# Half-width second diagonal scores, read back turned, with grouped gate logits and new lags, in a fused attention and mixture-of-experts kernel

## The chip, the cores and the metric

The kernel runs on one core of one Trainium2 chip. The metric is the device time of one execution in microseconds (us), taken as the median of several runs. Lower is better.

## The reference, cut to what matters

For each of 8 batches, with 2496 tokens, a width of 256 and keys of width 64, the attention part is

```python
scores = scale * np.matmul(z, z.transpose(0, 2, 1))
attn = np.maximum(scores, 0.0) ** 2
x = u * np.matmul(attn, v)
```

Queries and keys are the same tensor `z`, so `scores` is symmetric. The second part is a mixture of 8 experts: `logits = x @ w_gate + bias`, the expert is the largest logit, and the output is its probability times `relu(x @ w1[e]) @ w2[e]` with a hidden width of 1024. All values are float32. The kernel splits each float32 operand of a product into a high and a low part in the matmul's reduced format and adds three products.

## The kernel before

**Phase 1 (attention and routing).** The queries of a batch are cut into 5 chunks `c` of 512 (the last has 448), and the keys into 10 key pairs `i` of 2 times 128. A step is one (batch, chunk, key pair). For a step, `scores` makes 6 matmuls from `z` into the one PSUM tile `s` (three pairs; the two matmuls of a pair work on 64 rows of the array each, side by side). ScalarE's `root` (ReLU with the scale) empties `s` into a tile `r`, `square` squares it in place, `high` rounds it to `ah` (on ScalarE or VectorE, as the planner decides), VectorE's `low` takes the rest `al`, and `weigh` makes 24 matmuls with `v` into four banks `acc`. After the last step of a chunk ScalarE's `evacuate_low` (a copy, `x<-acc`) and VectorE's `evacuate_high` empty the banks, `weigh_u` multiplies by `u`, `turn_rows`, `store_rows` and `load_natural` bring the rows into token order through HBM, and `make_gates` makes 8 small matmuls `pg` per chunk (each recorded as two), which `take_gates` turns into the logits `lg`. After the fifth chunk of a batch the tokens are routed and scattered to HBM by expert.

Since scores are symmetric, a block below the diagonal is not computed twice: after a step above the diagonal `turn_squares` (VectorE) turns the squared block, `store_squares` writes it to HBM, and a later chunk reads it with `load_turned` in place of scores, root and square. Steps with `i // 2 == c` are the diagonal: both key pairs of the diagonal were computed at the full 512 queries.

**The order of the work** comes from a planner in the kernel. Each piece of work has an engine, an estimated time, a due step (`need`), and buffers that it takes and drops; the planner plays them through on its own clocks and writes each engine's instructions down in the order that results. All DMAs of phase 1 but the scatters go through SP's one queue in that order. `load_v` and `prep_v_high` (the cast `vh<-vr`) prepare `v` of the next batch while the present one runs.

**Phase 2 (experts)** has its order written out by hand: `up`, `down_both`, `down_high` for tiles of 512 tokens, with weights fetched in quarters into tiles of the pool `x`.

Of the kernel before, what the change touches and what calls it, by code (L numbers as in the profile page):

```python
# [16 lines left out]
P = 128  # L17
# [10 lines left out]
def tile_attention_moe(ctx: ExitStack, tc: tile.TileContext, ut, v, zt, mid, wg, mb, w1, w2, out):  # L28
# [35 lines left out]
    NA = 6  # L64
# [6 lines left out]
    xs = dram.tile([E * CAP, XW], F32, name="xs")  # L71
    natural = {(b, c): dram.tile([P, P // BLK, J, QB], F32, name=f"rows{b}_{c}") for b in range(B) for c in range(NCH)}
# [16 lines left out]
    rows.tile([P, 16], F32, name="room")  # L89
# [58 lines left out]
    def make_blank():  # L148
        t = rows.tile([P, J, XW], F32, tag="x", bufs=NCH + 1, name="blank")
        nc.gpsimd.memset(t, 0.0)  # L150
        blank.append(t)
# [135 lines left out]

    def scores(g, more=False):
# [14 lines left out]
        st_s[g] = s if more or not g else both  # L303

    def root(g):
        w = width[steps[g][1]]
        s = st_s.pop(g)
        r = bulk.tile([P, 2, T], F32, tag="a", bufs=NA, name="r") if g else first_root
# [12 lines left out]
    def turn_squares(g):  # L321

        b, c, i = steps[g]
        y = raw.tile([P, T // QB, 2, QB], F32, tag="turn", bufs=2, name="turn")
# [24 lines left out]
    def split_view(g, x):  # L349

        w = width[steps[g][1]]
        if is_turned(g):
# [3 lines left out]
    def split_out(g, x):  # L356
# [3 lines left out]
        return x.rearrange("p t (x n) -> p t x n", n=QB) if is_turned(g) else x  # L360

    roots = {}

    def square(g):
        w = width[steps[g][1]]
        a = r = st_s.pop(g)
        if g < 2:
# [112 lines left out]
    def evacuate_low(b, c, h):  # L480

        if not h:
            x = oT[b, c] = rows.tile([P, J, XW], F32, tag="x", bufs=NCH + 1, name="x")
# [16 lines left out]
    def turn_rows(b, c, h):  # L500

        if not h:
            pool, tag, n = (rows, "x", NCH + 1) if (b, c) == (B - 1, NCH - 1) else (raw, "turn", 2)
# [13 lines left out]
    def load_natural(b, c):  # L517

        x = X[b, c] = rows.tile([P, J, XW], F32, tag="x", bufs=NCH + 1, name="x")
# [5 lines left out]
    def make_gates(b, c):  # L525

        y = gates[b, c] = bank_tile([P, P], "pg")
        for h in range(KD):
            for j in range(J):
                nc.tensor.matmul(  # L530
                    out=y[j * BLK:(j + 1) * BLK], lhsT=gate_w[:, h], rhs=oT[b, c][:, j, h * P:(h + 1) * P],
                    start=h == 0, stop=h == KD - 1, tile_position=(0, j * BLK),
                )

    def take_gates(b, c):

        if c == 0:
            LG[b] = rows.tile([P, NCOL, BLK], F32, tag="lg", bufs=2, name="lg")
        y = gates.pop((b, c))
        nc.vector.transpose(  # L540
            out=LG[b][:, c * J:(c + 1) * J, :], in_=y.rearrange("p (t i) -> p t i", i=BLK)
        )
        oT.pop((b, c))
# [271 lines left out]
    def fetch_weights(t, quarters=range(4)):  # L815
# [4 lines left out]
        for q in quarters:  # L820
            x = rows.tile([P, F], F32, tag="x", bufs=NCH + 1, name="wr")
# [82 lines left out]

    def piece(on, us, need, f, *args, after=(), take=(), drop=(), gate=-1):
        p = Piece(on, us, need, f, args, [d if isinstance(d, tuple) else (d, 0.1) for d in after if d], list(take), drop, gate)
# [4 lines left out]
        "s": 1, "bank": 6, "a": NA, "ah": DEPTH, "al": DEPTH, "turn": 2, "zm": NCH + 1, "vh": 6, "vl": 6,  # L911
        "zr": 3, "vr": 3, "x": NCH + 1, "u": 1,
    }
    LEAD = 3.6
    LANES = 8
# [19 lines left out]
    def z_pieces(b, c):  # L935
# [5 lines left out]
        high = piece("A", 0.55, need - 1, prep_z_high, b, c, after=[read], take=[hold_z[b, c]], gate=int(need - 4))  # L941
# [627 lines left out]
```

## Time and profile before

| | |
|---|---|
| median of 3 runs | 2137.29 us (2137.05 to 2138.04) |
| profiled execution: its own time | 2140.08 us |
| profiled execution: its span, first to last instruction | 2138.3 us |
| TensorE (PE) busy | 2120.4 us, 99% of the span |
| VectorE (DVE) busy | 1591.4 us, 74% |
| ScalarE (ACT) busy | 1295.9 us, 61% |
| granted TensorE clock over the span | 0.996 |

The profiled execution took 2.8 us longer than the median of the runs, and 1.8 us of it lie outside the span. An engine's busy time counts its own instructions; for PE the ends of matmuls are modelled, since a matmul starts before the one ahead has drained. So what one matmul costs is read from start to start, not from its length.

### The profile page before, as it was taken

The page shows a single profiled execution, that of the slowest core. Times are in us where ns is not written, and L with a number is a line of the kernel's source. Part 1 is how long each engine was busy: PE and PEld are TensorE (multiplying, and loading weights), DVE is VectorE, ACT ScalarE, POOL GpSimd, SP SyncE. Part 2 cuts the span into 40 slices and gives each one's busy share as a digit, 9 for nine tenths or more (in the row PEclk, how much of TensorE's full clock was granted, in tenths as well). Part 3 has the DMA queues.
Part 4 walks back from the last instruction along what each step waited for, and adds up shares of the span by engine and source line. Part 5 has one row for each costly group of instructions (what it writes and reads, how often), then busy time and mean ns, then how long its engine had stood idle before and what let it go on. Part 6 is the DMA issues. An engine that isn't in the chain of part 4 may idle for free.

```text
span 2138.3 us, 42822 instructions
## 1 busy us (share of the span) xinstructions
PE 2120.4 (99%) x15910; PEld 1784.8 (83%) x15910; DVE 1591.4 (74%) x2464; ACT 1295.9 (61%) x1618; POOL 358.2 (17%) x343
## 2 busy tenths in 40 slices
PE   9999999999999999999999999999999999999997
PEld 7878888888888888888888888888888888888886
DVE  8778879878879888888787776666566666656664
ACT  9559668658658567567577643455454545545453
POOL 0001301301301201202104204112121111212112
PEclk9999999999999999999999999999999999999999
DMA  7987977987878878968878765545455454545541
GB/s 181 263 256 169 270 227 171 262 226 179 256 213 202 262 191 216 280 166 224 269 174 227 233 151 152 151 121 159 138 147 150 131 161 120 158 138 148 149 124 41
DMA packets 535403, 398.68 MB, mean 186 GB/s; under 512 B 317968, under 2 KB 469520, under 8 KB 535184
## 3 DMA queue, kind: packets, MB, share of 16 engines
q1 hardware_dynamic: 519968, 354.78, 62.1%
q0 software_dynamic: 15216, 41.08, 5.6%
q8 instruction: 126, 2.06, 0.4%
q14 instruction: 93, 0.76, 0.1%
HBM read 250.68 MB, written 145.16 MB: 185 GB/s over the span
## 4 chain that ended last, share of the span: by engine, by line
PE 97%; ACT 1%; DVE 1%; DMA 0%; issue 0%; POOL 0%; POOLq 0%; SPq 0%; ACTq 0%
PE acc L431 48%; PE ph L1247 19%; PE po L1265 13%; PE s L302 8%; PE po L1271 7%; PE pg L530 1%; ACT r L310 0%; DMA vr<-in_v_dram 0%; ACT r L373 0%; PE warm L1125 0%; DVE hl L1252 0%; PE ph L1345 0%; DMA rows<-turn 0%; ACT ah L396 0%; POOL out_dram L1285 0%
## 5 line engine op out<-in xcount | busy, mean ns | idle before, releaser
L431 PE MATMUL acc<-ah,vh 64*128 64x512 f32 (+1 forms) x3120 | 447.9, 386 | 3.3 <-ACT x L487 2.5
L405 DVE TENSOR_TENSOR al<-r,ah 128x1024 fp32r<-128x1024 f32 (+1 forms) x359 | 421.5, 1182 | 30.7 <-ACT ah L396 26.5
L431 PE MATMUL acc<-al,vh 64*128 64x512 f32 (+1 forms) x3120 | 434.5, 382 | 0.0
L431 PE MATMUL acc<-ah,vl 64*128 64x512 f32 (+1 forms) x3120 | 433.2, 383 | 0.0
L1252 DVE SCALAR_TENSOR_TENSOR hl<-ph,hh 128x512 fp32r<-128x512 f32 x312 | 210.3, 689 | 270.4 <-ACT hh L1251 270.3
L310 ACT ACTIVATE r<-s 128x1024 f32<-128x1024 f32 (+2 forms) x244 | 247.0, 1013 | 250.2 <-PE s L302 247.1
L1247 PE MATMUL ph<-xh,w 128*128 128x512 f32 x1248 | 398.5, 390 | 0.0
L431 PEld LDWEIGHTS acc<-ah,vh 64*128 64x128 f32 x3120 | 303.6, 185 | 67.5 <-issue 7.7
L648 POOL DMA_INDIRECT xs<-x,sloti x160 | 200.7, 1254 | 911.5 <-DMA squares<-turn 394.6
L431 PEld LDWEIGHTS acc<-al,vh 64*128 64x128 f32 x3120 | 307.4, 184 | 51.1
L431 PEld LDWEIGHTS acc<-ah,vl 64*128 64x128 f32 x3120 | 300.5, 185 | 53.0
L1251 ACT ACTIVATE hh<-ph 128x512 fp32r<-128x512 f32 x312 | 181.3, 595 | 264.9 <-PE ph L1247 263.5
L396 ACT CAST ah<-r 128x1024 fp32r<-128x1024 f32 (+1 forms) x268 | 272.9, 1032 | 83.8 <-PE acc L431 47.1
L1265 PE MATMUL po<-w,hh 128*128 128x512 f32 x1248 | 296.2, 389 | 0.0
L1247 PEld LDWEIGHTS ph<-xh,w 128*128 128x128 f32 x1248 | 234.6, 188 | 47.8 <-issue 0.3
L1265 PEld LDWEIGHTS po<-w,hh 128*128 128x128 f32 x1248 | 234.0, 188 | 48.3
L1285 POOL DMA_INDIRECT out_dram<-y,ids x157 | 152.7, 973 | 670.8 <-DVE y L1319 645.4
L329 DVE STREAM_TRANSPOSE turn<-r 128x512 f32<-128x512 f32 x316 | 205.4, 689 | 76.4 <-DMA squares<-turn 42.1
L373 ACT ACTIVATE r<-r 128x1024 f32<-128x1024 f32 (+2 forms) x243 | 255.8, 1053 | 6.7
L1247 PE MATMUL ph<-xl,w 128*128 128x512 f32 x624 | 243.7, 391 | 0.0
L302 PE MATMUL s<-zm 64*128 64x512 f32 (+1 forms) x1452 | 212.2, 392 | 1.8 <-ACT r L310 1.5
L847 DVE TENSOR_TENSOR w<-wr,w 128x1024 fp32r<-128x1024 f32 x148 | 174.5, 1219 | 11.5 <-ACT w L842 11.5
(157 smaller groups left out, 1703.6 us busy)
## 6 DMA issues: line engine op xcount, KB each, us to landing
wr<-in_moe_w_dram SPq DMA_DIRECT2D x148, 512.0 KB
squares<-turn SPq DMA_DIRECT2D x508, 128.0 KB
r<-squares SPq DMA_DIRECT2D x96, 512.0 KB
r<-squares SPq DMA_DIRECT2D x62, 448.0 KB
ut<-in_ut_dram SPq DMA_DIRECT2D x40, 512.0 KB
rows<-turn SPq DMA_DIRECT2D x160, 128.0 KB
x<-rows SPq DMA_DIRECT2D x160, 128.0 KB
xg<-xs SPq DMA_DIRECT2D x156, 128.0 KB
```

The source lines that it names most:

```text
L302: nc.tensor.matmul(out=s[t][:, :w], lhsT=lhs, rhs=mv[halves[t], ql, :w], start=n == 0, stop=n == 2)
L310: nc.scalar.activation(out=r[:, t, :w], in_=s[t][:, :w] if g < 2 else s[:, :, :w], func=AF.Relu, scale=INV)
L329: nc.vector.transpose(out=dst[:, n], in_=src[:, n])
L373: nc.scalar.square(out=a[:, t, :w], in_=r[:, t, :w])
L396: copy(out=split_out(g, ah), in_=split_view(g, st_a[g]))
L405: nc.vector.tensor_tensor(out=split_out(g, al), in0=split_view(g, a), in1=split_out(g, ah).bitcast(F32), op=ALU.subtract)
L431: nc.tensor.matmul(out=acc[b, c][r][dh][:, :w], lhsT=V[b, k // J][y][halves[r], k % J, dh * P:(dh + 1) * P], rhs=x[halves[r], k % 2, :w], ...
L648: nc.gpsimd.indirect_dma_start(out=xs, out_offset=bass.IndirectOffsetOnAxis(ap=RT[b]["sloti"][:n, k:k + 1], axis=0), in_=x[:n, j, :], in_o ...
L1247: nc.tensor.matmul(out=ph, lhsT=lhs, rhs=rhs[:, k, :], start=n == 0, stop=n == 3 * KD - 1)
L1251: nc.scalar.activation(out=hh, in_=ph, func=AF.Relu)
L1252: nc.vector.scalar_tensor_tensor(out=hl, in0=ph, scalar=0.0, in1=hh.bitcast(F32), op0=ALU.max, op1=ALU.subtract)
L1265: nc.tensor.matmul(out=PO[t][j], lhsT=hh, rhs=both, start=f == 0, stop=False, skip_group_check=True)
```

## The change

- **Half diagonal.** On the diagonal of chunks 0 to 3 (all but the very first chunk of the first batch) the second key pair forms scores for 256 queries only. The other 256 columns are the first key pair's block, turned: after the first pair's square, VectorE's `turn_corner` makes two transposes of half size, `store_corner` four DMAs of 64 KB to HBM, and `load_corner` one DMA of 256 KB back into the tile of the second step, into which `root` and `square` then write their half. `order_of` puts the first diagonal pair first among a chunk's fresh steps and the second last.
- **Logits in groups.** `make_gates` and `take_gates` run for chunks (0, 1, 2) and (3, 4) at once; in the last batch for (0), (1), (2, 3) and (4).
- **Accumulation of a chunk's first two steps** is interleaved: first half of step 1, first half of step 2, second half of step 1, second half of step 2 (each half writes two of the four banks).
- **The planner** gets other due times (`LAGS`), waits a little longer for some pieces (`SLACK`), and other estimates. Pools: one `a` tile more (7), three `turn` tiles in place of two, five `x` tiles in place of six.
- For a whole batch the last chunk's turned rows, the routing and the loads of rows come some steps later.

```diff
+        if c < NCH - 1 and (b or c):
+            fresh = [2 * c] + [i for i in fresh if i // 2 != c] + [2 * c + 1]
...
+    def on_diagonal(g, half):
+
+        b, c, i = steps[g]
+        return c < NCH - 1 and i == 2 * c + half and b + c > 0
...
+        q = slice(H, T) if on_diagonal(g, 1) else slice(0, w)
+        n_of = q.stop - q.start
...
-                nc.tensor.matmul(out=s[t][:, :w], lhsT=lhs, rhs=mv[halves[t], ql, :w], start=n == 0, stop=n == 2)
+                nc.tensor.matmul(out=s[t][:, :n_of], lhsT=lhs, rhs=mv[halves[t], ql, q], start=n == 0, stop=n == 2)
...
+        if on_diagonal(g, 1):
+            a = st_a.pop(g)
+            nc.scalar.activation(
+                out=a[:, H // QB:].rearrange("p x t n -> p t x n"),
+                in_=both_of(s)[:, :, 0:H].rearrange("p t (x n) -> p t x n", n=QB), func=AF.Relu, scale=INV,
+            )
...
+    def load_corner(g):
+
+        b, c, i = steps[g]
+        a = st_a[g] = bulk.tile([P, T // QB, 2, QB], F32, tag="a", bufs=NA, name="r")
+        nc.sync.dma_start(out=a[:, 0:H // QB], in_=corners[c, b % 2])
+
+    def turn_corner(g):
+
+        y = raw.tile([P, H // QB, 2, QB], F32, tag="turn", bufs=3, name="turn")
+        dst = y.rearrange("p t r (i n) -> p n r t i", n=2)
+        src = st_a[g][:, :, H:T].rearrange("p n (t i r) -> p n r t i", i=BLK, r=2)
+        for n in range(2):
+            nc.vector.transpose(out=dst[:, n], in_=src[:, n])
...
+    def store_corner(g):
+
+        b, c, i = steps[g]
+        y = st_t.pop(g)
+        dst = corners[c, b % 2].rearrange("(t i) x r n -> i t x r n", i=BLK)
+        for n in range(P // BLK):
+            nc.sync.dma_start(out=dst[:, :, n], in_=y[n * BLK:(n + 1) * BLK])
...
+    def group_of(b, c):
+        splits = ((0, 1, 2), (3, 4)) if b < B - 1 else ((0,), (1,), (2, 3), (4,))
+        return next(x for x in splits if c in x)
...
+        elif second:
+            a_us, a_take, a_drop = begun_half.pop((b, c))
+            p = piece("P", us / 2, n - 0.5, weigh, n, 0, after=ready)
+            p = piece("P", a_us, n, weigh, n - 1, 1, after=[(p, 0.0)], take=a_take, drop=a_drop)
+            weighed[n - 1] = p
+            p = piece("P", us / 2, n + 0.5, weigh, n, 1, after=[(p, 0.0)], drop=hold_h + v_of)
```

The next rows are PE's, in the third batch, from the first steps of a chunk to the next gate logits and scores (`s` scores, `acc` weigh, `pg` gate logits). Before:

```order
L431 MATMUL acc<-al,vh 128x512 x4
L431 MATMUL acc<-ah,vh 128x512 x8
L431 MATMUL acc<-ah,vl 128x512 x8
L431 MATMUL acc<-al,vh 128x512 x8
L431 MATMUL acc<-ah,vh 128x512 x8
L431 MATMUL acc<-ah,vl 128x512 x8
L431 MATMUL acc<-al,vh 128x512 x8
L530 MATMUL pg<-x,gate_w 32x128 x8
L431 MATMUL acc<-ah,vh 128x512 x8
L431 MATMUL acc<-ah,vl 128x512 x8
L431 MATMUL acc<-al,vh 128x512 x8
L302 MATMUL s<-zm 128x512 x6
```

The same engine and place in the changed kernel:

```order
L482 MATMUL acc<-al,vh 128x512 x4
L482 MATMUL acc<-ah,vh 128x512 x4
L482 MATMUL acc<-ah,vl 128x512 x4
L482 MATMUL acc<-al,vh 128x512 x4
L482 MATMUL acc<-ah,vh 128x512 x8
L482 MATMUL acc<-ah,vl 128x512 x8
L482 MATMUL acc<-al,vh 128x512 x8
L582 MATMUL pg<-x,gate_w 32x128 x24
L482 MATMUL acc<-ah,vh 128x512 x8
L482 MATMUL acc<-ah,vl 128x512 x8
L482 MATMUL acc<-al,vh 128x512 x8
L315 MATMUL s<-zm 128x256 x6
```

The gate logits of three chunks stand in one block, the second halves of two steps follow each other, and the scores of the second diagonal step have 256 columns. In all, 31 of the scores blocks have 256 columns, and the 40 blocks of gate logits become 18.

The next rows are ACT's, in the first batch, around the copies that empty the banks of its third chunk (`x<-acc`). Before:

```order
L232 CAST vh_1573<-vr_1476 128x1024
L310 ACTIVATE r_1600<-s_1566 128x1024
L373 ACTIVATE r_1600<-r_1600 128x1024
L396 CAST ah_1632<-r_1600 128x1024
L487 COPY x_1664<-acc_1220 128x4x128
L396 CAST ah_1668<-r_1524 128x1024
L487 COPY x_1664<-acc_1261 128x4x128
L310 ACTIVATE r_1680<-s_1670 128x1024
```

The same place in the changed kernel:

```order
L447 CAST ah_1555<-r_1402 128x1024
L334 ACTIVATE r_1599<-s_1566 128x1024
L424 ACTIVATE r_1599<-r_1599 128x1024
L447 CAST ah_1607<-r_1599 128x1024
L447 CAST ah_1630<-r_1522 128x1024
L538 COPY x_1650<-acc_1239 128x4x128
L538 COPY x_1650<-acc_1285 128x4x128
L447 CAST ah_1667<-r_1550 128x1024
```

The cast of the next batch's `v` no longer stands ahead of these copies; the first such cast comes after the copies of the fourth chunk. Over the kernel, 69 of the casts `ah<-r` go from DVE to ACT (ACT has 337 of them where it had 268, DVE 61 where it had 130).

The last rows are PE's in the last batch of the changed kernel, at the second block of gate logits:

```order
L482 MATMUL acc<-al,vh 128x512 x8
L315 MATMUL s<-zm 128x512 x6
L582 MATMUL pg<-x,gate_w 32x128 x8
L315 MATMUL s<-zm 128x256 x6
L482 MATMUL acc<-ah,vh 128x512 x8
```

Two scores blocks stand there with only a block of gate logits between them; before, weigh matmuls lay between any two scores blocks after the opening of the kernel.

## Rows read from the trace of the kernel before

**Rows 1.** Page, parts 1 and 4: busy time and share; chain by engine.

```profile
PE 2120.4 (99%) x15910; PEld 1784.8 (83%) x15910; DVE 1591.4 (74%) x2464; ACT 1295.9 (61%) x1618; POOL 358.2 (17%) x343
PE 97%; ACT 1%; DVE 1%; DMA 0%; issue 0%; POOL 0%; POOLq 0%; SPq 0%; ACTq 0%
```

**Rows 2.** Windows: one batch, and phase 2 with the end of phase 1; start:end, length, busy (xcount).

```profile
240.30:395.80 155.50, 155.47 (x1438) 129.00 (x1436) 126.74 (x196) 111.19 (x122) 25.37 (x21) 1.00 0.82 219
...
1250.00:2138.30 888.30, 876.51 (x4520) 749.99 (x4516) 570.78 (x867) 432.10 (x670) 164.47 (x169) 0.99 0.48 138
```

**Rows 3.** Waits of PE, 84.7 to 1173.6: us in total, times, longest.

```profile
PE acc L431 <- ACT x L487: 2.5, 2, 1.6
```

**Rows 4.** Waits of PE's weight loads (PEld), 240.3 to 1173.6, six batches.

```profile
PEld s L302 <- ACT r L310: 2.7, 7, 0.5
```

**Rows 5.** PE's timeline around a scores block: start, length, instruction, xcount.

```profile
253.92 0.86 PE L302 MATMUL s<-zm 64*128 64x512 f32 x6
254.62 1.07 PE L431 MATMUL acc<-ah,vh 64*128 64x512 f32 x8
255.53 1.07 PE L431 MATMUL acc<-ah,vl 64*128 64x512 f32 x8
```

**Rows 6.** PE's timeline in phase 2: matmuls of 256 columns, and the next.

```profile
1507.40 2.08 PE L1271 MATMUL po<-w,hl 128*128 128x256 f32 x16
1509.31 0.40 PE L1247 MATMUL ph<-xh,w 128*128 128x512 f32 x1
```

**Rows 7.** PEld's timeline around a routing count: weight loads in quick succession.

```profile
347.91 0.19 PEld L612 LDWEIGHTS pc<-cnt,ones 64*128 64x128 f32 x2
348.02 0.54 PEld L302 LDWEIGHTS s<-zm 64*128 64x128 f32 x6
```

**Rows 8.** PE's timeline around one block of gate logits.

```profile
246.96 0.86 PE L302 MATMUL s<-zm 64*128 64x512 f32 x6
247.76 0.65 PE L530 MATMUL pg<-x,gate_w 128*32 128x128 f32 x16
248.33 1.20 PE L431 MATMUL acc<-ah,vh 64*128 64x512 f32 x8
249.37 1.08 PE L431 MATMUL acc<-ah,vl 64*128 64x512 f32 x8
```

**Rows 9.** Lines by form, PE: the gate logits over the kernel.

```profile
L530 PE MATMUL pg<-x,gate_w 128*32 128x128 f32 x640 | 25.9, 279 | 0.0
```

**Rows 10.** PE's timeline at a chunk's end in the first batch.

```profile
108.70 0.86 PE L302 MATMUL s<-zm 64*128 64x512 f32 x6
111.17 0.50 PE L431 MATMUL acc<-ah,vh 64*128 64x512 f32 x1 [1.61 <-ACT x L487]
112.60 1.22 PE L431 MATMUL acc<-ah,vh 64*128 64x512 f32 x3 [0.93 <-ACT x L487]
...
119.46 0.85 PE L431 MATMUL acc<-ah,vh 64*128 64x512 f32 x5
```

**Rows 11.** Windows: the stretch behind it, with PE's granted clock.

```profile
112.60:118.30 5.70, 5.70 (x26) 4.50 (x28) 5.67 (x8) 2.97 (x3) 0.00 (x0) 0.50 0.71 184
```

**Rows 12.** ACT's timeline in the same stretch.

```profile
106.49 1.05 ACT L232 CAST vh<-vr 128x1024 fp32r<-128x1024 f32 x1 [6.65 <-DMA vr<-in_v_dram]
...
111.96 0.59 ACT L487 COPY x<-acc 128x512 f32<-128x512 f32 x1
```

**Rows 13.** Lines of ACT and of DVE, 240.3 to 395.8 (one batch).

```profile
L310 ACT ACTIVATE r<-s 128x1024 f32<-128x1024 f32 (+1 forms) x30 | 30.7, 1022 | 32.9 <-PE s L302 32.8
...
L329 DVE STREAM_TRANSPOSE turn<-r 128x512 f32<-128x512 f32 x40 | 26.0, 689 | 13.0 <-ACT r L373 6.9 <-DMA squares<-turn 5.9
L396 DVE CAST ah<-r 128x1024 fp32r<-128x1024 f32 (+1 forms) x13 | 8.7, 675 | 7.7 <-ACT r L373 6.8 <-PE acc L431 0.9
```

**Rows 14.** DMA, 240 to 396: packets and bytes.

```profile
DMA packets 51591, 34.13 MB, mean 219 GB/s; under 512 B 27530, under 2 KB 46602, under 8 KB 51574
```

**Rows 15.** Waits of all engines, 240.3 to 1173.6: casts of turned blocks.

```profile
ACT ah L396 <- DMA r<-squares: 16.9, 8, 4.5
```

More of the change, by code (lines that the diff above doesn't have):

```diff
@@ L71, in tile_attention_moe @@
     xs = dram.tile([E * CAP, XW], F32, name="xs")
+    corners = {(c, e): dram.tile([P, H // QB, 2, QB], F32, name=f"corner{c}_{e}") for c in range(NCH - 1) for e in range(2)}
     natural = {(b, c): dram.tile([P, P // BLK, J, QB], F32, name=f"rows{b}_{c}") for b in range(B) for c in range(NCH)}
@@ L148, in make_blank @@
     def make_blank():
-        t = rows.tile([P, J, XW], F32, tag="x", bufs=NCH + 1, name="blank")
+        t = rows.tile([P, J, XW], F32, tag="x", bufs=NCH, name="blank")
         nc.gpsimd.memset(t, 0.0)
@@ L986, in step_pieces @@
                 "D" if own else "AD", 1.3 if own else 0.93 * f, n - 1.8, high, n,
-                after=[high_after, split.get("high")], take=[Hold("ah")],
+                after=[high_after, split.get("high"), (high_first, 0.2) if half else None], take=[Hold("ah")],
                 drop=[Hold("a")] if n == 1 else (),
@@ L998, in step_pieces @@
             p = piece(
[L999 removed]
+                "D", 1.09 * f + 0.05, n - 1.1, low, n, after=[(p, 0.12), split.get("low")], take=hold_h[1:], drop=[hold_a],
             )
@@ L1010, in step_pieces @@
         us = (2.74 if i < NI - 1 else 2.05) * f
+        second = steps[n - 1] == (b, c, first_step[b, c]) and n - 1 > 0
         if first and n:
             p = piece("P", us / 2, n, weigh, n, 0, after=ready, take=own[0])
-            p = piece("P", us / 2, n, weigh, n, 1, after=[(p, 0.0)], take=own[1], drop=hold_h + v_of)
+            begun_half[b, c] = us / 2, own[1], hold_h + v_of
+        elif second:
[4 more added lines that the diff above has]
+            p = piece("P", us / 2, n + 0.5, weigh, n, 1, after=[(p, 0.0)], drop=hold_h + v_of)
         else:
@@ new lines, in chunk_pieces @@
+        cs = group_of(b, c)
+        made = weighted.setdefault((b, cs), [])
+        made.append((x, hold_o))
+        if c == cs[-1]:
+            p = piece(
+                "P", 0.35 + 0.43 * len(cs), end + later_by + 2.6, make_gates, b, cs,
+                after=[done_once["gate"]] + [(x, 0.15) for x, _ in made], take=[hold_g], drop=[h for _, h in made],
+            )
+            p = piece("D", 0.1 + 0.13 * len(cs), end + later_by + 3.2, take_gates, b, cs, after=[(p, 0.25)], drop=[hold_g])
+            for k in cs:
+                taken[b, k] = [p]
@@ L1056, in chunk_pieces @@
         whole = c == NCH - 1 and b < B - 1
         if whole or b == B - 1 and c == 1:
-            route_pieces(b, WHOLE if whole else SOON, end + (4 if whole else 2), [p for k in range(c + 1) for p in taken[b, k]])
+            route_pieces(b, WHOLE if whole else SOON, routed_at(b) if whole else end + 2, [p for k in range(c + 1) for p in taken[b, k]])
     def route_pieces(b, cols, need, after):
@@ L1168, in fits @@
                 need[h.pool] = need.get(h.pool, 0) + 1
-            if p.f in (load_turned, root) and free["a"] <= sum(n not in held for n in range(step_now + 1, p.args[0])):
+            if p.f in (load_turned, load_corner, root) and p.take and free["a"] <= sum(n not in held for n in range(step_now + 1, p.args[0])):
                 return False
```

145 lines of the change are left out of this document (93 added, 52 removed).

## The prediction

> **What bounds the kernel now.** I read the page first, then windows of one batch, then PE's waits and its timeline. PE is busy 99% of the span, and 97% of the chain that ended last is PE's own work [rows 1]. In a batch of 155.5 us PE is busy for 155.47, while DVE has 126.74, ACT 111.19 and the DMA engines 0.82 of it [rows 2]. From batch 1 on PE waits for nobody for any time that a list of its waits shows: the only entry from 84.7 to 1173.6 is 2.5 us behind ACT's bank copies, and it falls in the first batch [rows 3, 10]. So matmul work taken away shortens phase 1 one for one, as long as no wait takes its place. Phase 2 (876.51 of 888.30 us busy) [rows 2] keeps its order; it loses one of six `x` tiles, but a quarter of weights is loaded right after the quarter of the tile before was used, so four tiles are held and a fifth is enough. I cost that at nothing.
>
> **Half scores.** A full scores block takes 254.62 - 253.92 = 0.70 us of PE, start to start [rows 5]. No row has 64-row pairs of 256 columns. The nearest are phase 2's matmuls of 256 columns, each with its own weight load: (1509.31 - 1507.40) / 16 = 0.119 us [rows 6]. A pair of 64-row matmuls runs side by side (8 of them take 255.53 - 254.62 = 0.91 us, 0.227 a pair [rows 5]), so three pairs cost 3 x 0.119 = 0.36 us. The bounds are 0.35 (half of 0.70) and 0.70 (nothing saved, if the pair's weight loads set the pace). I take 0.36, since weight loads of 64 rows also start 0.11 us behind the pair before [rows 7]. There are 31 such blocks: 31 x 0.34 = 10.5 us less (0 to 10.9).
>
> The Trainium skill, TensorE: Matmul & The Clock Gate, sections LDWEIGHTS (loading the stationary operand) and The mechanism, speaks against this: a load of 128 columns takes 128 / 1.2 = 107 ns whatever its rows, and it overlaps a running matmul only in another row group. Successive pairs here use the same two row groups, so by that rule a pair would cost load plus columns, as an estimate from that page 3 x (107 + 109) ns = 0.65 us, and the edit would give 1.6 us. The trace does not agree: matmuls of all rows with a load each go every 0.119 us [rows 6].
>
> **Gate logits in groups.** One block of before costs more than its own stretch: the scores ahead take 0.80 in place of 0.70, the block 0.57, and the eight matmuls behind 1.04 in place of 0.91 [rows 5, 8]. Together 0.80 us. A further chunk in the same block pays only for its matmuls. The block is busy 0.65 us and one instruction lasts 0.28 [rows 8, 9], so its first and last starts lie 0.37 apart; four run side by side, which makes three spacings of 0.12 and 0.49 us for four rounds. Each merged chunk saves 0.31 us (0.23 if it costs the whole 0.57). 40 blocks become 18, so 22 are merged: 6.8 us less (5.1 to 7.3).
>
> **Chunk starts.** Before, a scores block stood between the two halves of a chunk's first step, and its weight loads waited for root to empty `s`: 7 times, 2.7 us in six batches [rows 4]. The new order has two halves there (24 matmuls, 2.7 us), longer than a root of 1.02 us [rows 13]. PE itself loses less than its loads wait; between 0 and 2.7 us I take half, 1.4 us less.
>
> **The stop in the first batch.** At 108.70 PE ran a scores block and then waited for ACT's bank copies [rows 10]. ACT had stood 6.65 us behind the cast `vh<-vr`, whose load was late, and the copies are behind that cast in its order [rows 12]. After the stop the granted clock was 0.50, that is 1.2 of 2.4 GHz, for 5.70 us [rows 11]. From 108.70 to 119.46 PE did one scores block and 36 matmuls, 0.70 + 18 x 0.227 = 4.8 us at its usual pace; 10.76 - 4.8 = 6.0 us were lost. In the new ACT order no cast of `v` stands ahead of these copies, so I take all 6.0 away (0 if another late transfer holds ACT there).
>
> **What the change adds.** Per corner DVE gets two transposes of half of 0.689 us [rows 13], 21 us in 31 corners, and loses 69 casts of 0.675 [rows 13], 47 us. ACT loses half of a root and of a square per corner (1.02 us by the root [rows 13], 32 us in all) and gains the 69 casts, as large as a root, 70 us: plus 38 us over eight batches, under 5 a batch on 111 of 155. Both stay below PE, so these cost nothing, unless the order goes wrong; an engine that is late once costs a stop as above. Four corners a batch move 4 x 0.5 MB on 34.13 [rows 14], 6% more, with the batch some 2% shorter: the DMA share goes from 0.82 to about 0.88. SP's queue gets five issues more per corner. A step whose corner is late would hold ACT's cast and all behind it, but turned blocks came up to 4.5 us late, eight times, without PE stopping [rows 15]. For transfers that do come too late I take 2.0 us (between 0 and one stop of 6.0): the nearest row, the 2.5 us of [rows 3], less the slower clock.
>
> In the last batch two scores blocks stand too close: one with only gate logits between, one with less than half a step's weigh. The second has to wait until `s` is empty: 0.86 us of block and a root of 1.02 make 1.88 from start to start [rows 5, 13], where the order gives 0.70 + 0.80 = 1.5. That is 0.4 us, some more where copies stand ahead of root. Bounds 0 and 3.8 (two whole such cycles); I take 1.2 us for both.
>
> **Sum.** -10.5 - 6.8 - 1.4 - 6.0 + 2.0 + 1.2 = -21.5 us. Against the profiled execution's own 2140.08 us this gives 2118.6; its median stands 2.8 us below it, so the runs should show 2115.8, and I say **2116**.
>
> **Rivals.**
> - *The stop stays or moves.* The first batch has the densest DMA traffic, with blank rows written as well. Another late load ahead of bank copies costs the 6.0 us again: 2122. For it speaks that ACT takes its work strictly in order; against it that the only load of that kind is gone from that place.
> - *Half blocks save nothing.* If the pair's loads set the pace, two loads one after the other at 0.11 [rows 7] make 0.22 a pair, as much as the 0.227 of now: -21.5 + 10.5 gives 2126. The page's rule above would end near this. Against it stands [rows 6].
> - *Transfers take back most of it.* Without the 2.0 us allowed above, the sum is -23.5; four stops of 6.0 us bring it to 2137.3 - 23.5 + 24 = 2137.8, no change. (A measurement of this kernel can tell about 0.2%, 4.3 us, from no change.) For it speaks the fuller DMA share; against it that the batches of before ran at some 0.82 without one stop after the first [rows 2, 3].
> - *Slower.* The corner's way is turn, four issues, store and load in SP's one queue, and ACT's cast of the half step waits for its end with the bank copies behind it. Should that be too late once in each of seven batches, as `vr` was in [rows 12], it costs 7 x 6.0 = 42 us: 2137.3 - 23.5 + 42 = 2155.8. It decides from five stops on (30 us against 23.5 + 4.3). Against it: at least five steps of 2.7 us lie between the two diagonal steps, and turned blocks with such a way come 4.5 us late at most [rows 15].
>
> **How the numbers follow.** My forecast 0.52 (2110 to 2119), the stop stays 0.24, half blocks save nothing 0.12, transfers take most 0.06, slower 0.06. The range 2110 to 2131 holds the first three; its low end has every term at its better bound (-10.9 - 7.3 - 2.7 - 6.0 and no cost for close scores or late loads: 2110.4), its high end the third with a stop kept. Faster by over 0.2% (below 2133.0): 0.88; within: 0.06; slower: 0.06.
>
> **What would show it.** In the profile of after, the 256-column scores take about 0.36 us start to start, a block of 24 gate matmuls about 1.4 us, a full batch about 155.5 - 4 x 0.34 - 3 x 0.31 - 0.2 = 153.0 us, PE has no wait behind `x<-acc` near 110 us, and the clock stays at 1.00 there. Phase 2 keeps its length. I am wrong if a batch of after is longer than 154 us, or if PE's list of waits names bank copies or casts behind corner loads several times, with granted clock below 1 behind each.

## The result, and the profile after

| | before | after |
|---|---|---|
| median of the runs | 2137.17 us (4 runs, 2135.98 to 2138.04) | 2117.67 us (4 runs, 2117.03 to 2118.48) |
| profiled execution: own time, span | 2140.08, 2138.3 us | 2118.48, 2116.7 us |
| ratio after / before | | 0.9909, 95% interval 0.9892 to 0.9927 |

The changed kernel is faster by 19.5 us. Its page, part 1 and the first line of part 4, answers to [rows 1]:

```profile
PE 2097.4 (99%) x15910; PEld 1777.1 (84%) x15910; DVE 1567.4 (74%) x2435; ACT 1333.5 (63%) x1687; POOL 348.6 (16%) x343
...
PE 94%; DMA 1%; DVE 1%; ACT 1%; issue 1%; SPq 0%; POOL 0%; POOLq 0%; DVEq 0%; ACTq 0%
```

PE still sets the time, but its own work is 94% of the chain where it was 97%: something else has come into it. The windows say where. The first is the place of the old stop in the first batch, the second one full batch, the third the last batch, the fourth phase 2 with the end of phase 1 ([rows 2, 11] of before; same columns):

```profile
104.00:118.00 14.00, 14.00 (x160) 11.36 (x158) 12.30 (x14) 8.14 (x10) 0.21 (x1) 1.00 0.77 223
240.00:392.50 152.50, 152.50 (x1438) 128.41 (x1436) 124.84 (x196) 113.69 (x129) 24.45 (x21) 1.00 0.88 240
1077.50:1238.00 160.50, 155.75 (x1448) 128.74 (x1448) 124.02 (x235) 108.03 (x122) 48.19 (x42) 1.00 0.84 230
1238.00:2116.70 878.70, 866.93 (x4428) 741.44 (x4424) 564.44 (x861) 425.27 (x663) 164.46 (x169) 1.00 0.49 137
```

PE is never idle at the old stop and has its full clock there. A full batch is 152.5 us with the DMA engines at 0.88. Of the seven batches after the first, only the last has idle PE: 160.5 - 155.75 = 4.75 us.

Cut at the first weigh matmul of each batch (each batch has 1170 of them in the trace), phase 1 looks like this, in us; the last column runs to the last weigh matmul. Each row is one profiled execution. The rows under the first two are the experiments of the next section.

| kernel | batch 0 | 1 | 2 | 3 | 4 | 5 | 6 | 7 |
|---|---|---|---|---|---|---|---|---|
| before | 163.20 | 156.07 | 155.60 | 155.63 | 155.64 | 155.62 | 154.95 | 155.29 |
| after | 154.66 | 152.57 | 152.53 | 152.51 | 152.49 | 152.55 | 152.54 | 160.59 |
| x1_full_columns | 155.59 | 153.89 | 153.89 | 153.87 | 153.84 | 153.91 | 153.90 | 161.74 |
| x2_single_gates | 158.83 | 152.82 | 154.30 | 152.76 | 154.24 | 152.89 | 153.64 | 166.36 |
| x4_no_corner | 155.96 | 153.80 | 153.82 | 153.13 | 153.87 | 154.63 | 153.18 | 157.73 |
| x3_before_gate1 | 157.93 | 156.04 | 155.61 | 155.62 | 155.69 | 155.60 | 154.92 | 155.64 |
| l1_group01 | 154.69 | 152.56 | 152.53 | 152.51 | 152.49 | 152.59 | 152.54 | 163.47 |
| l2_route16 | 154.68 | 152.56 | 152.53 | 152.51 | 152.49 | 152.55 | 152.54 | 159.94 |
| l3_route16 | 154.54 | 152.53 | 153.20 | 152.51 | 152.49 | 152.55 | 152.54 | 158.11 |
| x6_double_store | 155.75 | 153.19 | 154.45 | 153.33 | 152.49 | 153.68 | 153.07 | 165.40 |
| m1_last_full | 154.67 | 152.53 | 152.53 | 152.51 | 152.49 | 152.55 | 152.54 | 160.08 |
| m2_last_full_route16 | 154.66 | 152.57 | 152.53 | 152.51 | 152.49 | 152.55 | 153.01 | 158.47 |
| n1_route28_16 | 154.64 | 152.57 | 152.53 | 152.51 | 152.49 | 152.55 | 159.16 | 155.43 |
| x5_plain_starts | 157.74 | 153.51 | 153.39 | 153.47 | 153.49 | 154.70 | 154.27 | 164.56 |

From before to after the first batch gives 8.5 us, the six in the middle 18.3 (3.05 each), and the last takes 5.3 back: 21.5, the difference of the two spans (21.6) within 0.1. From the last weigh matmul to the last of PE it is 866.9 us in both, so phase 2 did not change.

The timeline of PE in after, at a scores block of 256 columns, at a block of three chunks' gate logits, and at a chunk's start (start, length, instruction, xcount), answers to [rows 5, 8]:

```profile
243.02 0.52 PE L315 MATMUL s<-zm 64*128 64x256 f32 x6
243.37 1.08 PE L482 MATMUL acc<-ah,vh 64*128 64x512 f32 x8
...
265.65 1.07 PE L482 MATMUL acc<-al,vh 64*128 64x512 f32 x8
266.65 1.53 PE L582 MATMUL pg<-x,gate_w 128*32 128x128 f32 x48
268.11 1.20 PE L482 MATMUL acc<-ah,vh 64*128 64x512 f32 x8
269.14 1.07 PE L482 MATMUL acc<-ah,vl 64*128 64x512 f32 x8
...
319.30 0.62 PE L482 MATMUL acc<-al,vh 64*128 64x512 f32 x4
319.76 0.86 PE L315 MATMUL s<-zm 64*128 64x512 f32 x6
320.46 0.39 PE L482 MATMUL acc<-ah,vh 64*128 64x512 f32 x2
```

The half block takes 243.37 - 243.02 = 0.35 us from start to start (0.36 was forecast). The gate block starts 266.65 - 265.65 = 1.00 after eight weigh matmuls that take 0.91, lasts 1.46 (about 1.4 was forecast), and the eight behind it take 1.03 in place of 0.91: 0.09 + 1.46 + 0.12 = 1.67 us for three chunks, where three blocks of before cost 3 x 0.80 = 2.4. At the chunk's start the scores block follows four weigh matmuls 0.46 us after their start, and takes 0.70: nothing is lost.

PE's waits in the last batch, 1100 to 1240 (us in total, times, longest); from 84 to 1100 the same list is empty, where [rows 3] had bank copies:

```profile
PE acc L482 <- DVE al L456: 1.4, 3, 0.9
PE s L315 <- ACT r L334: 1.4, 2, 0.9
PE pg L582 <- DVE x L549: 1.2, 2, 1.0
PE pc L667 <- DVE x L542: 0.3, 1, 0.3
PE pc L667 <- DVE cnt L658: 0.3, 1, 0.3
PE s L315 <- ACT r L326: 0.2, 1, 0.2
```

These are 4.8 us in ten short waits behind DVE and ACT. What those two had waited for in the same stretch stands in the waits of all engines:

```profile
ACT ah L447 <- DMA r<-squares: 17.6, 5, 7.3
DVE turn L353 <- DMA squares<-turn: 8.5, 4, 3.4
DVE turn L353 <- DMA rows<-turn: 4.5, 1, 4.5
```

In the last batch of before (1104 to 1260) the first of these reads

```profile
ACT ah L396 <- DMA r<-squares: 8.6, 2, 4.5
```

So turned blocks that came late held ACT for twice as long in the last batch of after. In that batch DVE also has the 25 small operations that route the batch before, at 1115 to 1126 us, where several of these short waits lie. Two theories of the last batch follow: its VectorE and ScalarE work (routing, four gate blocks), or its transfers. The timelines of ACT and DVE show that a good part of the waits leads back to transfers:

```profile
1124.19 1.04 ACT L447 CAST ah<-r 128x1024 fp32r<-128x1024 f32 x1 [1.37 <-DMA r<-squares]
```

```profile
1133.15 1.31 DVE L353 STREAM_TRANSPOSE turn<-r 128x512 f32<-128x512 f32 x2 [2.73 <-DMA squares<-turn]
```

Behind that cast comes the root for which a scores block waits 0.91 us, and behind those transposes the rest `al` for which weigh waits 0.86. The counts of the routing itself (`pc`) account for 0.6 us of the 4.8.

### The profile page after: what moved, and what is told of

Read it like the earlier page. It is cut to its first block, busy times and chain, and to the rows that moved or that the text cites. A ratio compares the mean times of both kernels' runs of the same rounds, so it can differ in the third digit from the quotient of the medians.

```text
span 2116.7 us, 43063 instructions
## 1 busy us (share of the span) xinstructions
PE 2097.4 (99%) x15910; PEld 1777.1 (84%) x15910; DVE 1567.4 (74%) x2435; ACT 1333.5 (63%) x1687; POOL 348.6 (16%) x343
## 4 chain that ended last, share of the span: by engine, by line
PE 94%; DMA 1%; DVE 1%; ACT 1%; issue 1%; SPq 0%; POOL 0%; POOLq 0%; DVEq 0%; ACTq 0%
PE acc L482 47%; PE ph L1355 20%; PE po L1373 13%; PE s L315 7%; PE po L1379 7%; PE pg L582 1%; DMA r<-squares 0%; ACT r L334 0%; DMA rows<-turn 0%; DVE turn L353 0%; DMA squares<-turn 0%; ACT ah L447 0%; DVE al L456 0%; ACT r L424 0%; PE warm L1233 0%
## 5 line engine op out<-in xcount | busy, mean ns | idle before, releaser
L447 ACT CAST ah<-r 128x1024 fp32r<-128x1024 f32 (+1 forms) x337 | 342.3, 1035 | 70.0 <-PE acc L482 42.6
L703 POOL DMA_INDIRECT xs<-x,sloti x160 | 191.1, 1194 | 947.3 <-DVE x L701 856.4
L482 PEld LDWEIGHTS acc<-al,vh 64*128 64x128 f32 x3120 | 301.1, 184 | 54.3 <-DVE al L456 2.9
L482 PEld LDWEIGHTS acc<-ah,vh 64*128 64x128 f32 x3120 | 297.7, 185 | 55.5 <-issue 2.4
L482 PEld LDWEIGHTS acc<-ah,vl 64*128 64x128 f32 x3120 | 294.2, 184 | 52.9
L334 ACT ACTIVATE r<-s 128x1024 f32<-128x1024 f32 (+2 forms) x213 | 215.2, 1011 | 164.9 <-PE s L315 164.9
L1393 POOL DMA_INDIRECT out_dram<-y,ids x157 | 152.7, 973 | 670.8 <-DVE y L1427 645.7
L424 ACT ACTIVATE r<-r 128x1024 f32<-128x1024 f32 (+2 forms) x212 | 222.8, 1051 | 5.7
L315 PE MATMUL s<-zm 64*128 64x512 f32 (+2 forms) x1452 | 198.2, 378 | 3.2 <-ACT r L334 2.9
```

Source lines behind the costliest of these rows:

```text
L315: nc.tensor.matmul(out=s[t][:, :n_of], lhsT=lhs, rhs=mv[halves[t], ql, q], start=n == 0, stop=n == 2)
L334: nc.scalar.activation(out=r[:, t, :w], in_=s[t][:, :w] if g < 2 else s[:, :, :w], func=AF.Relu, scale=INV)
L424: nc.scalar.square(out=a[:, t, :w], in_=r[:, t, :w])
L447: copy(out=split_out(g, ah), in_=split_view(g, st_a[g]))
L482: nc.tensor.matmul(out=acc[b, c][r][dh][:, :w], lhsT=V[b, k // J][y][halves[r], k % J, dh * P:(dh + 1) * P], rhs=x[halves[r], k % 2, :w], ...
L703: nc.gpsimd.indirect_dma_start(out=xs, out_offset=bass.IndirectOffsetOnAxis(ap=RT[b]["sloti"][:n, k:k + 1], axis=0), in_=x[:n, j, :], in_o ...
```

## The experiments

Each was timed against the kernel before, whose medians beside them are 2137.02 to 2137.68 us. A difference from the changed kernel is that of the medians, and of the profiled executions where batches are named.

### x1_full_columns: only the columns

```diff
-        q = slice(H, T) if on_diagonal(g, 1) else slice(0, w)
+        q = slice(0, w)
...
-                in_=both_of(s)[:, :, 0:H].rearrange("p t (x n) -> p t x n", n=QB), func=AF.Relu, scale=INV,
+                in_=both_of(s)[:, :, H:T].rearrange("p t (x n) -> p t x n", n=QB), func=AF.Relu, scale=INV,
```

> The changed kernel, but the scores of the 31 second diagonal steps form all 512 columns again, and the ReLU reads the upper 256 of them; the mirrored 256 are still read back turned. What it tells apart: whether the columns left out are worth TensorE time, or were hidden. If TensorE pays for every column, each of the 31 steps has a block longer by 4 x (0.70 - 0.353) us, as the rows of both traces have 0.70 for a score pair of 512 columns and 0.353 for one of 256; the prediction counted it as one block of 0.34 a step: 31 x 0.346 = +10.7 us over the changed kernel, near 2128, and the steady batches would be 1.4 us longer (152.5 to 153.9). If the time came from elsewhere (the groups, the waits of VectorE and ScalarE), it is within 3 us of 2117.7.

Measured: 2127.60 us (2127.31 to 2128.33), 9.9 above after, ratio to before 0.9955 (0.9939 to 0.9972). Each steady batch grew by 1.32 to 1.36 us, 0.34 for each of its four half steps (the expectation's "4 x" holds for a batch, not for a step). PE's timeline in x1, the same place as the half block above:

```profile
244.28 0.86 PE L315 MATMUL s<-zm 64*128 64x512 f32 x6
244.98 1.07 PE L482 MATMUL acc<-ah,vh 64*128 64x512 f32 x8
```

PE pays for the columns; the rival that half blocks save nothing is out.

### x2_single_gates: logits one chunk at a time

```diff
-        splits = ((0, 1, 2), (3, 4)) if b < B - 1 else ((0,), (1,), (2, 3), (4,))
+        splits = tuple((k,) for k in range(NCH))
```

> The changed kernel with the gate logits of each chunk in a block of their own again (5 a batch in place of 2). Theory: a block of 8 gate matmuls between score blocks costs a switch each, so a batch goes from 2.88 us of such blocks to about 4.1, by the rows of both traces; 7 x 1.2 = +8.5 us, near 2126, the steady batches at 153.7. Rival: the merged blocks saved nothing by themselves, the shorter steady batches come from the scores alone: 2117.7 within 2 us.

Measured: 2131.45 us (2128.73 to 2134.49), 13.8 above after, ratio 0.9971 (0.9961 to 0.9982). The six steady batches have a mean of 153.44, that is 0.91 above after, or 0.30 for each of the three blocks that were merged. (The order of steps moved too, so that single batches have one scores block more or less.) That is the size of the prediction's 0.31, and less than the 1.2 a batch that was expected of this run. The other 10 us of the profiled execution lie in the first batch (4.2, with one scores block more and a wait of 1.1 us behind root) and in the last (5.8), which the expectation did not foresee.

### x5_plain_starts: a chunk's first two steps not interleaved

```diff
-            begun_half[b, c] = us / 2, own[1], hold_h + v_of
-        elif second:
+            p = piece("P", us / 2, n, weigh, n, 1, after=[(p, 0.0)], take=own[1], drop=hold_h + v_of)
+        elif False:
```

> The changed kernel with the two halves of a chunk's first step one piece after the other again, not interleaved with the second step's; half steps, groups and lags stay, and the planner orders the rest anew. The steady batches fell by 3.1 us; 1.37 are the half steps and 0.9 the groups by the runs so far, 0.8 are left. If the 0.8 are the chunk starts (the prediction sized them at 0.2 a batch), a steady batch without a stop goes from 152.5 to about 153.3; by the prediction's size it is 152.7. The whole time also holds the stops that the planner's new order brings and tells little of this.

Measured: 2132.36 us (2131.24 to 2134.09), ratio 0.9975 (0.9965 to 0.9985). The batches 1 to 3, in which PE waits for nobody, are at 153.39 to 153.51, 0.9 above after. (Batch 4 has a wait of 0.8 us and one scores block fewer.) PE's timeline of x5 at a chunk's start:

```profile
319.33 0.62 PE L482 MATMUL acc<-ah,vl 64*128 64x512 f32 x4
319.79 0.62 PE L482 MATMUL acc<-al,vh 64*128 64x512 f32 x4
320.44 0.97 PE L315 MATMUL s<-zm 64*128 64x512 f32 x6
321.25 0.63 PE L482 MATMUL acc<-ah,vh 64*128 64x512 f32 x4
```

The scores block begins 0.65 us after the start of four weigh matmuls that take 0.46, and takes 0.81 in place of 0.70. That is 0.3 us at this chunk start, 0.19 of waiting and 0.11 of a slow restart; in after both are gone. Compared with after chunk by chunk, the five starts of a batch lose about 0.3, 0, 0.1, 0.2 and 0.3 us.

### x3_before_gate1: the stop in the first batch, in the kernel before

```diff
-            high = piece("A", 0.95, need - 1.5, prep_v_high, b, c, after=[read], take=hold_v[b, c][:1])
+            high = piece("A", 0.95, need - 1.5, prep_v_high, b, c, after=[read], take=hold_v[b, c][:1],
+                gate=at_step[0, 2, NI - 1] + 1 if b == 1 else -1)
```

> The kernel before, with the ScalarE casts of V of batch 1 held back until the last step of its chunk 2 has been issued, so that in the first batch they stand behind the copies that free the score banks. Theory of the prediction: the stop of 5 to 6 us in the first batch came from one cast that waited for its DMA in front of such a copy: 2137.2 - 6 = about 2131, with the first batch near 157. Rival: ScalarE would have been held by another late DMA, and the stop moves: 2137 within 1 us, the first batch at 163.

Measured: profiled execution 2134.57 us against 2140.08, its first batch 157.93 against 163.20, all others alike within 0.4. PE's timeline at the place of [rows 10], and the windows' row of 104 to 118:

```profile
108.08 0.86 PE L302 MATMUL s<-zm 64*128 64x512 f32 x6
108.78 0.39 PE L431 MATMUL acc<-ah,vh 64*128 64x512 f32 x1
109.67 0.73 PE L431 MATMUL acc<-ah,vh 64*128 64x512 f32 x3 [0.50 <-ACT x L487]
```

```profile
104.00:118.00 14.00, 13.50 (x126) 10.90 (x124) 11.28 (x14) 8.26 (x10) 0.00 (x0) 1.00 0.86 248
```

In these two executions the cast was the cause: without it in front of the copies the wait is 0.50 us and the clock stays at 1.00. The medians say less: 2135.16 (about 2131 was expected; 10 runs, 2134.22 to 2138.05) against 2137.48 (19 runs, 2134.00 to 2140.87), ratio 0.9994 (0.9985 to 1.0004), which does not tell it from no change. The runs of before reach from a time without the stop to one a little above the profiled execution, so it looks as if the stop had a different size in each execution; this is argued from their times alone, and x3 without the cast in front of the copies still has a run of 2138.05.

### x4_no_corner and m1_last_full: the corners' transfers

x4 has no half steps at all; m1 has none in the last batch.

```diff
 x4
-        return c < NCH - 1 and i == 2 * c + half and b + c > 0
+        return False
 m1
-        return c < NCH - 1 and i == 2 * c + half and b + c > 0
+        return c < NCH - 1 and i == 2 * c + half and 0 < b * NCH + c < (B - 1) * NCH
```

> The changed kernel without the half steps: the second diagonal step of each chunk is a full step of 512 columns as before, and the corner isn't read back, so its DMA traffic falls by 16 MB. The grouped logits and the other lags stay. Theory of the prediction (its terms: half scores -10.5, late transfers +2.0): 2117.7 + 10.5 - 2.0 = 2126, with the last batch shorter by what the corner's transfers cost it. If the last batch of the changed kernel is long (160.6 us in place of 152.5) because of the DMA traffic, that batch falls to about 155 here and the total is near 2123; if it is long by the routing's VectorE operations, it stays near 161 and the total is 2128.

> The changed kernel without half steps in its last batch alone: four of the 31 corners go, with 1.8 MB of transfers, and four scores blocks have 512 columns again. TensorE's own work in that batch grows by 4 x 0.346 = 1.4 us. Theory that the last batch of the changed kernel (160.6 us in place of 152.5) is long because its DMA engines carry 36.9 MB where the kernel before had 31.9: it falls to about 157 to 158, as in the run with no corner at all, and the time to 2114.5 to 2116. Theory that the corners' traffic matters through the batches ahead (0.88 of the DMA engines, against 0.82 before): 161 to 162, and the time near 2119. Theory of the routing's VectorE operations alone: 162, near 2119.

Measured: x4 2123.23 us (2122.74 to 2123.85), ratio 0.9934 (0.9918 to 0.9951); m1 2116.64 us (2115.35 to 2118.11), ratio 0.9904 (0.9888 to 0.9921). In x4 the last batch falls by 2.9 us although PE has 1.4 more to do, so 4.2 us went with the corners (their transfers, and their transposes on DVE too). x4's total is that of the theory of the DMA traffic, its last batch, 157.73, lies between the two. In m1, which drops the same corners of the last batch, it falls by 0.5 only, 1.9 without PE's own 1.4, and none of the theories of m1 gives its 160.08. Both move 34.9 MB in that batch where after moves 36.9, so the amount moved is not what sets them apart. PE's waits in m1's last batch do fall, from 4.8 to 2.2 us, but 1.4 of them are one more stop behind the bank copies, and the clock fell with it:

```profile
1113.00:1119.00 6.00, 4.62 (x27) 3.41 (x25) 4.56 (x15) 4.52 (x7) 0.00 (x0) 0.72 0.56 73
```

### x6_double_store: each corner stored twice

```diff
+    again = {(c, e): dram.tile([P, H // QB, 2, QB], F32, name=f"again{c}_{e}") for c in range(NCH - 1) for e in range(2)}
...
+        dst = again[c, b % 2].rearrange("(t i) x r n -> i t x r n", i=BLK)
+        for n in range(P // BLK):
+            nc.sync.dma_start(out=dst[:, :, n], in_=y[n * BLK:(n + 1) * BLK])
```

> The changed kernel, which stores each corner a second time to another place in DRAM that nothing reads: the 31 corners' store traffic is doubled and their SyncE issues too. Theory that the DMA engines have room in the steady batches and that only the last batch is short of them: steady batches 152.5 within 0.3 us, the last batch 1 to 4 us longer, total 2118 to 2122. Theory that the transfers are nearly critical throughout (the rival of the prediction in which they take most of it back): 10 us or more longer. Theory that the last batch is long by VectorE's routing and the gate blocks alone: 2117.7 within 1 us.

Measured: 2132.14 us (2128.51 to 2135.10), 14.5 above after, ratio 0.9973 (0.9964 to 0.9983). The last batch takes 4.8 us more, and five of the six batches in the middle 0.5 to 1.9 more. That is over the 0.3 us that the first theory left to the steady batches, and the total is that of the second, in which transfers are nearly critical throughout. In the middle (170 to 1080) the waits now have

```profile
ACT vh L234 <- DMA vr<-in_v_dram: 18.7, 6, 4.7
...
ACT ah L451 <- DMA r<-corner: 4.7, 5, 2.2
...
PE acc L486 <- ACT ah L451: 0.8, 1, 0.8
```

where the first of these in after is

```profile
ACT vh L233 <- DMA vr<-in_v_dram: 5.9, 5, 2.2
```

The casts that wait for a corner are not what reaches PE: in each of the five batches PE loses most of its time ahead of that cast. PE's one wait of 0.8 us, at 414.28, stands behind the kind of cast that made the old stop, again with a late load of `v`:

```profile
410.08 1.05 ACT L234 CAST vh<-vr 128x1024 fp32r<-128x1024 f32 x1 [4.70 <-DMA vr<-in_v_dram]
```

In the last batch one stop of 4.50 us makes the difference. These are the issues on SP, then ACT, then PE:

```profile
1125.38 2.94 SPq L413 DMA_DIRECT2D again<-turn  x4
1128.42 0.39 SPq L343 DMA_DIRECT2D r<-squares  x1
```

```profile
1132.44 1.04 ACT L451 CAST ah<-r 128x1024 fp32r<-128x1024 f32 x1 [3.46 <-DMA r<-squares]
```

```profile
1134.46 1.01 PE L316 MATMUL s<-zm 64*128 64x256 f32 x6 [4.50 <-ACT r L335]
```

SP issued the load of a turned block only after the four extra stores; the cast that waits for the load stands in front of the root for which the scores block waits. A copy that nobody reads makes others late, here by its place in SP's one queue.

### l1_group01, l2_route16, l3_route16: gate blocks and routing of the last batch

l1 is the first edit, l2 the second, l3 both.

```diff
-        splits = ((0, 1, 2), (3, 4)) if b < B - 1 else ((0,), (1,), (2, 3), (4,))
+        splits = ((0, 1, 2), (3, 4)) if b < B - 1 else ((0, 1), (2, 3), (4,))
...
-        return at_step[b, NCH - 1, NI - 1] + (36 if b < B - 2 else 5)
+        return at_step[b, NCH - 1, NI - 1] + (36 if b < B - 2 else 16)
```

> The changed kernel, with the gate logits of the last batch in three groups (chunks 0 and 1, 2 and 3, 4) in place of four. Theory that the last batch is long (160.6 us, others 152.5) by its own gate blocks: one block less, -1.2 to -2 us. Theory that it is long by the routing of the batch before, whose 25 small VectorE operations stand between the ReLU sums and these groups: no more than -0.5 us. Theory of the DMA traffic: no change.

> The changed kernel, with the routing of the last batch but one put off by 11 more steps (16 in place of 5 after its last step), groups as they are. Theory of the routing: the PE gaps at 1111 to 1126 us, 3 to 4 us in all, fall away: 2114 to 2116. Theory of the DMA traffic: the scatters start later and collide with the end of the batch: 2117 to 2121. Theory that the gate blocks themselves cost it: no change.

> Both edits: routing put off by 11 steps and the last batch's logits in three groups. Theory of the routing and the blocks together: 2112.5 to 2115. Theory of the DMA traffic: 2117 to 2121.

Measured: l1 2122.28 us (2121.15 to 2123.10), ratio 0.9933 (0.9916 to 0.9949); l2 2116.31 (2112.71, 2114.92, 2117.71, 2117.78), ratio 0.9898 (0.9881 to 0.9915); l3 2116.90 (2112.30, 2116.19, 2117.62, 2118.19), ratio 0.9902 (0.9883 to 0.9921). One gate block less made it 4.6 us worse, which no theory expected. The executions of l2 and l3 spread over the ranges of both theories and below. With the routing moved, all ten short waits of PE between 1111 and 1173 us were gone, and one stop stood at 1178. The timeline of l2 on PE, then on ACT:

```profile
1178.25 0.39 PE L482 MATMUL acc<-ah,vh 64*128 64x512 f32 x1
1182.68 1.22 PE L482 MATMUL acc<-ah,vh 64*128 64x512 f32 x3 [4.04 <-ACT x L538]
```

```profile
1181.10 1.04 ACT L447 CAST ah<-r 128x1024 fp32r<-128x1024 f32 x1 [5.36 <-DMA r<-squares]
1182.05 0.58 ACT L538 COPY x<-acc 128x512 f32<-128x512 f32 x1
```

It is the old stop in a new place: a cast whose data were late stands ahead of the copies that free the banks. The granted clock behind it was 0.50, and SP had issued the load at 1177.02, 1.3 us after ACT was free for the cast (1181.10 - 5.36 = 1175.74), behind eight loads of the rows that the moved routing asks for:

```profile
1182.00:1187.00 5.00, 4.32 (x20) 3.47 (x22) 4.43 (x6) 3.66 (x5) 0.97 (x1) 0.50 0.98 249
```

```profile
1168.41 8.52 SPq L572 DMA_DIRECT2D x<-rows  x8
1177.02 0.45 SPq L342 DMA_DIRECT2D r<-squares  x1
```

The waits of l1 in its last batch (1100 to 1245) have a bank copy that itself waits:

```profile
ACT x L538 <- DMA squares<-turn: 6.3, 1, 6.3
...
PE acc L482 <- ACT x L538: 4.6, 2, 3.7
```

The copy writes a tile of the pool `x`, and the semaphores that it waits for are those of scatters and of SP's transfers. By the trace the last to come was that of a scatter of rows, issued at 1146.69 and landed at 1153.13; the copy started at 1153.61. (The view names another transfer, a store.) So the copy waited for a free `x` tile. l1 keeps the tiles of chunks 0 and 1 until one common block of logits, and the change had taken the pool from six tiles to five. No run gives the sixth back, so what it is worth in the last batch is not known.

The theory of the routing is not refuted by l2. The short waits went with the routing, and the new stop, 4.04 us and a clock of 0.50 behind it, took back nearly all: the batch was 0.7 us shorter in the profiled execution. The fastest executions of l2 and l3 (2112.71 and 2112.30) are 5 us below after's median; whether they lack the stop, no trace shows.

### m2_last_full_route16 and n1_route28_16: both together, and an earlier routing

m2 is the edit of m1 with that of l2. n1 is after with

```diff
-        return at_step[b, NCH - 1, NI - 1] + (36 if b < B - 2 else 5)
+        return at_step[b, NCH - 1, NI - 1] + (36 if b < B - 3 else 28 if b < B - 2 else 16)
```

> The same, and the routing of the last batch but one put off by 11 steps. With the routing put off alone, nine short stops of 7.7 us together gave way to one of 5.0 us, at 1178 us, behind a turned block that came late, and single executions lay between 2112.7 and 2117.8. If that one is a matter of the DMA engines, it goes here, and the time is 2112 to 2114.5 in every execution. If it comes from the place of the routing, it stays: 2117 to 2119 in part of the executions.

> The changed kernel with its corners, the routing of the last batch but two 8 steps (some 27 us) earlier (28 in place of 36 steps), and that of the last batch but one 11 steps later (16 in place of 5), so that some 8 of the 12 scatters that the change had moved into the last batch go back to the batch ahead, 1 MB and the loads of their rows with it. Theory that the last batch is long by its amount of transfers: it falls to 154 to 157, the batch ahead stays at 152.5 to 153.5, and the time is 2110 to 2115. Theory that all batches are nearly full of transfers: the batch ahead gets the stop (up to 5 us longer), and the time stays at 2115 to 2119.

Measured: m2 2114.74 us (2114.54 to 2116.75), ratio 0.9897 (0.9881 to 0.9914); n1 2121.28 (2119.82 to 2124.00), ratio 0.9932 (0.9914 to 0.9950). m2 lies between its two theories, n1 above both of its. (The list of after has ten short waits of 4.8 us together, where the expectation of m2 says nine and 7.7.) In n1 the last batch is as short as before's (155.43), and the batch ahead is 6.6 us longer. The timeline of PE there, and what stood behind it in the waits of 1060 to 1076:

```profile
1073.56 1.34 PE L482 MATMUL acc<-ah,vh 64*128 64x448 f32 x8 [4.08 <-DVE ah L447]
```

```profile
DVE ah L447 <- DMA r<-squares: 6.5, 1, 6.5
```

The stop moved with the scatters, and again a turned block was late. m2 was the fastest median of all kernels here: no stop behind bank copies stands in its last batch (PE waits 1.2 us at 1198 to 1201 for nothing that the profile names), and its four executions lie below the four of after. But the 2.9 us between them are 0.14%, under what a measurement of this kernel can tell, and the two intervals overlap.

## Why the prediction came out

**The bound.** That PE's own work sets phase 1, and that matmul work taken away shortens it one for one, held up to the last batch: the list of PE's waits is empty from 84 to 1100 us, and the steady batches of x1 and x2 gave the time back. It did not hold in the last batch.

**Half scores: -10.5.** Right. A block takes 0.35 us, and x1 measured 9.9 us for 31 of them in the medians, 31 x 0.34 = 10.5 by its steady batches. The Trainium skill, TensorE: Matmul & The Clock Gate, section LDWEIGHTS (loading the stationary operand), sets the time of a load by its columns alone. With that page's section The mechanism, where a load overlaps only a matmul of another row group, the estimate for three pairs had been 0.65 us. The trace does not agree: 0.35.

**Gate logits in groups: -6.8.** Right: 0.30 us a merged block in the steady batches of x2 against 0.31, so 22 x 0.30 = 6.6.

**Chunk starts: -1.4.** Mis-sized. x5 gives 0.9 us a batch, and what x1 and x2 leave of the 3.05 is 0.8: 6 to 7 us in all if the first and last batch are counted alike. The step that failed is "PE itself loses less than its loads wait": I read only the wait in front of the scores block and halved it, and left out that the block then starts slowly (0.81 for 0.70). That explains a part only; x5 loses time at starts where its list shows no wait, and where the kernel before lost the rest is not shown start by start.

The three together are 1.35 + 0.91 + 0.9 = 3.2 us a batch; after is 3.05 shorter than before. The prediction had 153.0 us for a batch, it is 152.5.

**The stop in the first batch: -6.0.** The mechanism is shown by x3. Of the profiled executions it is 5.3 us. In the medians it is 2.3, which is not clear of noise. A stop that is smaller in most executions would explain why the forecast of the median missed more than that of the profiled execution: 2140.08 - 21.5 = 2118.6 stands against a measured 2118.48, but the 2.8 us between that execution and the median, which I took over unchanged, is not there in after, whose profiled execution lies only 0.8 above its median of 2117.67. This is argued, not shown.

**What the change adds: +2.0 and +1.2.** Mis-sized. The busy times moved as forecast (ACT +37.6 us for 38, DVE -24.0 for -26, the DMA share 0.88), but the last batch would have come to 155.29 - 1.4 - 0.3 - 0.9 = 152.7 by the three savings and took 160.59: 7.9 us, where the prediction had 3.2 for close scores and late transfers together. Close scores blocks did wait, twice, with a gate block between them: 0.45 us behind root, as the prediction said, and 0.91, which is more by a turned block that came 1.37 us late in front of root. The rest looks like the rival "transfers take back most of it" in small: not in every batch, but in the last one. [rows 15] could not show it, since that list ends where the last batch is half done. By the prediction's own sign, a batch longer than 154 us, it was wrong here: the last batch took 160.6 us.

So two errors of some 5 us cancelled, the chunk starts against the last batch, and that is luck. The sum -21.5 was right for the profiled execution, and the forecast of 2116 is 1.7 us under the median.

**What stays open** is why the transfers come late in the last batch. The amount moved does not decide: l2 moves the same 36.88 MB there as after, and m1, with 34.9, gained little. Nor does a transfer take longer there: in after the loads of turned blocks take a median of 5.6 us from issue to landing in the last batch (7.0 at most), and 5.2 to 5.6 in the six batches ahead (8.3 at most). The late ones were issued late. ACT's two longest waits for a turned block in that batch (5.7 and 7.3 us) ended with loads that SP issued 0.1 and 2.4 us after ACT was free for the cast, and in l2 and x6 the load stood behind the issues of other transfers in SP's one queue. What another order in that queue, or the sixth `x` tile, would give was not run; most new orders here brought another stop.

## What to carry to other kernels

Price a small block of other matmuls by three numbers: its own stretch, the wait in front of it, and the slow start of what comes next; here the last two were some 0.2 of the 0.30 us that a merged block saved. When an in-order engine holds buffers that TensorE waits for, look at what stands in front of the release and may be late, above all a load: one cast moved was worth 5.3 us of a profiled execution. Where all transfers go through one queue, look also at what is issued ahead of the load. And a profiled execution that lies above the median may do so because of the very stall that is removed, so don't carry its distance over to the changed kernel.

## What the runs showed of the hardware

- In a scores block a pair of 64-row matmuls with 256 columns goes every 0.35 / 3 = 0.118 us, and with 512 columns every 0.70 / 3 = 0.233, each with its own loads of weights: half the columns take half the time, so the loads do not show.
- After a block of gate logits, eight weigh matmuls take 1.03 us in place of 0.91, and the block itself starts 0.09 late; this costs the same whether the block has one chunk's matmuls or three.
- A store of 1 MB a batch (16 DMAs of 64 KB) that nothing depends on made five of six batches 0.5 to 1.9 us longer, at a DMA share of 0.89 to 0.91 where it had been 0.86 to 0.89.
- A load of a turned block (448 or 512 KB) took a median of 5.2 to 5.6 us from issue to landing in every batch of after from the second on, late or not.
- SP took 8.5 us to issue eight loads of rows in l2, and 2.9 us to issue four stores of 64 KB in x6; in both, the load of a turned block that came late was issued right behind them.
- The runs of the kernel before reach from 2134.0 to 2141.7 us, those of after from 2117.0 to 2118.5.
